# First batch's filter loop without weight conversions: six weight pieces joined in the first quads, first rows read back in two parts

## The chip, the cores and the metric

The kernel runs on one core of a Trainium2 chip. The metric is the device time of one execution in microseconds (us), as the median of several runs. A profile of one further execution comes with it; its times are counted from its first instruction.

## What is computed

The reference mixes each sequence with a filter in the frequency domain and passes the result through a two-layer network with ELU between the layers:

```python
x: (8, 3008, 256)   filt_r, filt_i: (1505, 256)
X = np.fft.rfft(x, axis=1)
y = np.fft.irfft(X * (filt_r + 1j * filt_i)[None], n=3008, axis=1)
h = y.reshape(24064, 256) @ w_in                      # w_in (256, 2048)
g = np.where(h > 0.0, h, np.exp(np.minimum(h, 0.0)) - 1.0)
out = (g @ w_out).astype(np.float32)                  # w_out (2048, 256)
```

The weights w_in and w_out are float64 in memory; the kernel turns them into float32 itself.

## The kernel before

**Batches, units and quads.** The sequence transform of a batch is written as small matrix products (3008 = 47 x 64) with transfers through DRAM between its stages. The network is computed in items (batch b, sixth m of its rows, quarter q of the hidden width): 8 x 6 x 4 of them. One turn of the last loop, here called a quad and numbered i, does the first layer of item i (seven "up" steps, `up_steps`) and the second layer of item i-1 (seven "down" steps, `down_steps`) in an interleaved order that is written out as a string of U and D. Both layers use a seven-product scheme for a 2x2 block product, so each weight quarter also needs four sums of its blocks (`w_sums`). The transform of batch b+1 is spread over the quads of batch b by a hand-written plan: `at(quad, place, fn, ...)` puts a call into a quad at place 2 (after the third step of its first half), place 0 (between the halves) or place 1 (at its end). Each engine runs its own instructions in program order, so a call stands in front of everything that the same engine is given later.

**The opening.** Batch 0 has nothing to overlap with, so it has its own code. Six `a_first` calls do its first transform; eight groups g of four `t_first` transposes, `b_first` and `bi_first` do the rest. `b_first(g)` makes two products on TensorE (PE) into two of the four PSUM banks psM (L329), then runs four products with the filter on VectorE (DVE, `products`, L333 to L336). `bi_first(g)` makes the inverse products (also L329) into psO and two ScalarE (ACT) evictions (L361, L362) into one of two buffers of `t3f`. `y_write_first(g)` (L369) writes that buffer to the DRAM tile `yds[0]`. In turn g of the loop, PE is given `b_first(g)`, `bi_first(g-2)` and, for g below 4, `t_first(g+4)`. When all eight are written, `y_read(0, 0)` (L466) reads the first rows, and `n_unit(0, 0)` (L479, L481) and `n_sums` (L505 to L508) make the input of quad 0.

**The weights.** There are 16 pieces k, four for each quarter q = k // 4: pieces 4q and 4q+1 are w_in, 4q+2 and 4q+3 are w_out. Quad i needs w_in of quarter i in its up steps; the down steps of quarter q run in quad q+1. A piece passes through `w_fetch` (DMA of the float64 words), `w_split` (two DVE operations, L699 and L700, mantissa and exponent bits), `w_float` (four ACT operations, L707, L708, L715, L716), `w_join` (three or four DVE operations, L722, L724, then L729 or L735) and, after the second of a pair, `w_sums` (four DVE operations, L743 to L746). `wtmp` holds two sets of temporaries, for even and for odd pieces.

Before the change pieces 0 to 6 are converted ahead of the loop over g. Inside it stand the float steps of 7 to 11, the joins of 7, 8, 9 and the splits of 8 to 11; in turn 7 follow the joins of 10 and 11 and the splits of 12 and 13; behind the loop, around `y_read`, the floats of 12 to 14, the split of 14 and the joins of 12 and 13. The join of 14 comes after `n_sums(0, 0)`, and piece 15 is converted in quads 0 to 3 of the plan.

**Queues.** GpSimd (POOL) issues the filter reads `ff<-fd` (L318) and most weight fetches, and after them, with no wait on the quads themselves, one memset (L211) and the filter copies `f_pairs` (L771 to L775) from DRAM to DRAM. SyncE (SP) issues the y writes and reads and, behind them, the rows of batch 1 (L202 to L213).

**In the quads.** `keep` (L541, ACT) copies a sum out of the PSUM bank phs, and the next up step adds into the same bank. `add` (L538, DVE) reads a bank and a kept copy; the fourth up step s4 adds into bank phd only after the DVE has read it for g["b22"]. `elu_exp` is L547 and L548 on ACT, `elu_max` is L552 on DVE, and four sums close the item (L588 to L592, DVE). `x_unit` (L219, L220, DVE) at place 0 of quads 2, 3 and 4 prepares batch 1.

Of the kernel before, what the change touches and what calls it, by code (L numbers as in the profile page):

```python
# [130 lines left out]
def kernel(  # L131
# [220 lines left out]
    def bi_first(g):  # L352
        s = ss.pop((0, g))
        t = t3s[0, g] = t3f[:, g % 2]
# [108 lines left out]
    def y_read(b, m, queues=(nc.sync, nc.sync)):  # L463
        t = t4s[b, m] = t4p.tile([P, 4, D], FP32, tag="t4", name="t4")
        for p in range(4):
            queues[p % 2].dma_start(t[p * 32:p * 32 + 32, :, :], yds[b][:, p * H + 4 * m:p * H + 4 * m + 4, :])  # L466

# [201 lines left out]
    def w_fetch(k, queue=nc.gpsimd):  # L669
# [6 lines left out]
        elif k in (6, 7, 8, 9):  # L676
            wd = xp.tile([P, 2, 2, D], FP32, tag="xc", name="wd").rearrange("p k u d -> p (k u d)")
        else:
            wd = fbufs[{5: 0, 12: 1, 13: 2, 14: 0, 15: 1}.get(k, k)].rearrange("p c u d -> p (c u d)")
# [14 lines left out]
    def w_split(k):  # L694
        m, e, c = wtmp[k % 2 if k < 15 else 0]
# [6 lines left out]
    def w_float(k, part=None):  # L702
        m, e, f, l = wts[k]
        if part == 1:
            return w_power(e)

        nc.scalar.activation(out=l, in_=wds[k][:, :, 0], func=AXT.Identity, scale=2.0 ** -52)  # L707
        nc.scalar.activation(out=f, in_=m, func=AXT.Identity, scale=2.0 ** -20, bias=1.0)  # L708
        if part is None:
            w_power(e)  # L710

    def w_power(e):

        ef = e.bitcast(FP32)
        nc.scalar.activation(out=ef, in_=e, func=AXT.Relu, scale=-8.0, bias=edges[:, 0:1])  # L715
        nc.scalar.activation(out=e, in_=ef, func=AXT.Relu, scale=-1.0, bias=edges[:, 1:2])  # L716

    def w_join(k):
# [17 lines left out]
        if j % 2 == 1 and k < 15:  # L736
            w_sums(k)
# [39 lines left out]
    with tc.manual_schedule():  # L777


        with tc.tile_pool(name="boot", bufs=1) as bp:  # L780
# [8 lines left out]
            t3f = t3p.tile([P, 2, 4, D], FP32, tag="t3", name="t3")  # L789
# [10 lines left out]
            for c in range(3):  # L800
# [8 lines left out]
                        [t1p.tile([P, XC, D], FP32, tag="t1", name="wfl").rearrange("p (a b) d -> p a (b d)", a=2)])  # L809
            for i, v in enumerate((1151.0 * 2 ** 23, 255.0 * 2 ** 23)):  # L810
# [30 lines left out]
            for g in range(NG):  # L841
                f_read_first(g, ff[:, g])
                if 3 <= g < 5:
                    w_fetch(g + 7)
            for k in (12, 13, 14):
                w_fetch(k)
            w_split(7)
            w_join(6)
            for g in range(4):
                t_first(g)  # L850
            for g in range(NG + 2):
# [7 lines left out]
                if g < 5:  # L859
                    w_float(g + 7)  # L860
                if g < 3:
                    w_join(g + 7)
                    w_split(g + 8)
                if g == 2:
                    w_split(11)
# [138 lines left out]
```

## Time and profile before

| what | value |
|---|---|
| median of 3 runs (lowest to highest) | 2607.95 us (2606.2 to 2610.34) |
| the profiled execution, its span | 2609.69 us, 2607.9 us |
| mean granted TensorE clock | 0.991 |
| busy share of the span: PE, DVE, ACT, POOL | 98%, 78%, 59%, 7% |
| first product of the filter loop (PE, L329) | 47.89 us |
| last product of the filter loop ends | 86.94 us |
| last eviction (ACT, L362) ends | 89.22 us |
| reads of the first rows issued (SP, ACT) | 92.28 us |
| first product of n_unit (PE, L479) | 96.84 us |
| first product of quad 0, 1, 2, 3, 4 | 100.39, 107.54, 121.09, 134.53, 148.10 us |

A line of the timeline has start, duration, engine, line and operation, output and input tiles, shapes and a count; brackets hold the idle time of that engine just before it and what ended it. A line of the windows has a stretch, then for PE, PE's weight loads (PEld), DVE, ACT and POOL the busy time and number of instructions, then the granted clock (1.00 is full speed), the share of the 16 DMA engines and GB/s. A line of the waits has who waited for whom, the total, the number of times and the longest. PE does one float32 product in two recorded passes.

### The profile page before, as it was taken

To read this page: it belongs to the slowest core of one execution; us is meant where nothing else is said; L and a number is where in the kernel's file an instruction comes from. 1 tells how busy PE (TensorE), PEld (TensorE's weight loads), DVE (VectorE), ACT (ScalarE), POOL (GpSimd) and SP (SyncE) were. 2 spreads that over 40 slices of the span, in tenths; PEclk is the share of its full clock that TensorE was granted. 3 is DMA by queue.
4 is the path that set the end of the run, shared out by engine and by line. 5 is a ranking of instruction groups with operands and counts; after the bars stand their busy time and mean duration, and the time that the engine had idled before them with its cause. 6 is when DMAs were issued, how large, how long until landed. Compare 5 with 4: busy or idle time off the path is not lost.

```text
span 2607.9 us, 39668 instructions
## 1 busy us (share of the span) xinstructions
PE 2549.2 (98%) x14460; PEld 2204.1 (85%) x14460; DVE 2046.0 (78%) x3538; ACT 1546.1 (59%) x2713; POOL 169.6 (7%) x333
## 2 busy tenths in 40 slices
PE   6799999999999999999999999999999999999998
PEld 4688889888898888988889888888888888898887
DVE  6878886788867888778876888778887688866666
ACT  7665655666556655665556556565655655555554
POOL 5100100010000000000000000000010001000000
PEclk8899999999999999999999999999999999999999
DMA  9663213422243231433215231243223322120010
GB/s 275 179 173 73 69 30 96 124 69 58 52 117 93 57 77 46 114 83 75 63 41 145 68 86 37 74 124 85 57 49 81 85 65 69 36 50 20 21 29 17
DMA packets 228834, 206.37 MB, mean 79 GB/s; under 512 B 130962, under 2 KB 194674, under 8 KB 228640
## 3 DMA queue, kind: packets, MB, share of 16 engines
q1 hardware_dynamic: 211328, 166.87, 26.2%
q0 software_dynamic: 15856, 36.25, 5.1%
q8 instruction: 114, 1.87, 0.3%
q10 hardware_dynamic: 1456, 0.72, 0.1%
q14 instruction: 80, 0.66, 0.1%
HBM read 131.87 MB, written 78.17 MB: 81 GB/s over the span
## 4 chain that ended last, share of the span: by engine, by line
PE 89%; DVE 6%; DMA 2%; ACT 1%; issue 1%; POOL 0%; DVEq 0%; ACTq 0%; POOLq 0%
PE po L612 41%; PE phs L530 23%; PE phd L530 12%; PE pha L530 6%; PE psn L479 3%; PE psa L233 1%; PE pf L382 1%; PE pv L445 1%; DVE g L538 1%; DVE g L552 1%; DMA fd<-in_filt_i_dram 1%; DMA t<-in_moe_w_out_dram 0%; ACT e L548 0%; ACT e L547 0%; DMA fd<-in_filt_r_dram 0%
## 5 line engine op out<-in xcount | busy, mean ns | idle before, releaser
L612 PE MATMUL po<-g,wo 128*128 128x256 f32 (+1 forms) x5376 | 1313.0, 376 | 0.0
L612 PEld LDWEIGHTS po<-g,wo 128*128 128x128 f32 x5376 | 1012.1, 190 | 163.2 <-issue 47.4
L541 ACT ACTIVATE g<-phs 128x512 f32<-128x512 f32 (+1 forms) x576 | 338.9, 588 | 766.9 <-PE phs L530 766.9
L538 DVE TENSOR_TENSOR g<-phd,g 128x512 f32<-128x512 f32 (+1 forms) x384 | 259.5, 676 | 302.9 <-ACT e L548 205.4
L548 ACT ACTIVATE e<-e 128x512 f32<-128x512 f32 (+1 forms) x768 | 477.2, 621 | 24.4
L530 PE MATMUL phs<-y,wi 128*128 128x256 f32 (+1 forms) x1536 | 388.8, 376 | 0.5
L530 PE MATMUL phs<-ys,wi 128*128 128x256 f32 (+1 forms) x1536 | 387.7, 375 | 1.5 <-ACT g L541 1.5
L552 DVE SCALAR_TENSOR_TENSOR g<-e,g 128x512 f32<-128x512 f32 (+1 forms) x576 | 386.9, 672 | 0.8 <-ACT e L548 0.2
L547 ACT ACTIVATE e<-g 128x512 f32<-128x512 f32 (+1 forms) x576 | 353.4, 614 | 48.7 <-DVE g L538 37.0
L530 PEld LDWEIGHTS phs<-ys,wi 128*128 128x128 f32 x1536 | 291.4, 190 | 35.4 <-ACT g L541 2.5
L530 PEld LDWEIGHTS phs<-y,wi 128*128 128x128 f32 x1536 | 287.6, 190 | 38.6 <-ACT fall L390 3.4
L552 DVE SCALAR_TENSOR_TENSOR g<-e,phs 128x512 f32<-128x512 f32 (+1 forms) x192 | 129.7, 676 | 138.5 <-ACT e L548 138.5
L530 PE MATMUL phd<-ys,wi 128*128 128x256 f32 (+1 forms) x768 | 195.3, 377 | 10.0 <-DVE g L538 10.0
L530 PE MATMUL phd<-y,wi 128*128 128x256 f32 (+1 forms) x768 | 193.7, 375 | 0.0
L530 PE MATMUL pha<-y,wi 128*128 128x256 f32 (+1 forms) x768 | 193.7, 375 | 0.0
L547 ACT ACTIVATE e<-phs 128x512 f32<-128x512 f32 (+1 forms) x192 | 113.0, 588 | 125.3 <-PE phs L530 125.2
L530 PEld LDWEIGHTS phd<-ys,wi 128*128 128x128 f32 x768 | 144.6, 190 | 31.6 <-DVE g L538 15.5
L530 PEld LDWEIGHTS pha<-y,wi 128*128 128x128 f32 x768 | 145.8, 190 | 16.5
L530 PEld LDWEIGHTS phd<-y,wi 128*128 128x128 f32 x768 | 145.8, 190 | 16.5
L323 POOL DMA_DIRECT2D fall<-fp x224 | 110.5, 501 | 702.6 <-DVE r L418 650.2
L538 DVE TENSOR_TENSOR g<-pha,g 128x512 f32<-128x512 f32 (+1 forms) x192 | 129.1, 672 | 25.2 <-PE pha L530 25.1
L592 DVE TENSOR_TENSOR g<-g,g 128x512 f32<-128x512 f32 (+1 forms) x192 | 130.7, 681 | 6.7
(138 smaller groups left out, 2117.2 us busy)
## 6 DMA issues: line engine op xcount, KB each, us to landing
yd<-t SPq DMA_DIRECT2D x127, 192.0 KB
t<-yd SPq DMA_DIRECT2D x190, 128.0 KB
z<-t SPq DMA_DIRECT2D x84, 256.0 KB
fall<-fp POOLq DMA_DIRECT2D x224, 96.0 KB, 2.9
t<-z SPq DMA_DIRECT2D x224, 96.0 KB
out_dram<-o SPq DMA_DIRECT2D x632, 32.0 KB
tn<-tn_t SPq DMA_DIRECT2D x48, 256.0 KB
xc<-in_x_dram SPq DMA_DIRECT2D x84, 128.0 KB
```

The costliest lines, as they stand in the source:

```text
L233: nc.tensor.matmul(p[o:o + 64, u, :], w[r, u, o:o + 64], src[r, u, :], start=True, stop=True)
L323: nc.gpsimd.dma_start(t[32 * a:32 * a + 24].rearrange("p c u d -> p (c u d)"), fp[g, a].rearrange("q c u d -> q (c u d)"))
L382: nc.tensor.matmul(pf[p][1][32 * a:32 * a + 32, js, :], fb[r, v, :], t2[r, js, a, :], start=True, stop=True, tile_position=(32 * p, 32 * a))
L479: nc.tensor.matmul(ps[:, ts(q, P)], t[:, i - 4 * m, ds(dh * P, P)], w[:, i - 4 * m, :], start=True, stop=True)
L530: nc.tensor.matmul(ps[:, a, 0:h], w_in[q][:, COMBO[n], a, :], y[n], start=start and a == 0, stop=True, skip_group_check=True)
L538: nc.vector.tensor_tensor(out=g[o], in0=i0, in1=i1, op=ALU.add)
L541: nc.scalar.activation(out=g[o], in_=i0, func=AXT.Copy)
L547: nc.scalar.activation(out=e, in_=src, func=AXT.Relu, scale=-1.0)
L548: nc.scalar.activation(out=e, in_=e, func=AXT.Exp, scale=-1.0)
L552: nc.vector.scalar_tensor_tensor(out=g[n], in0=es[n], scalar=1.0, in1=src, op0=ALU.subtract, op1=ALU.max)
L592: nc.vector.tensor_tensor(out=g["t4"], in0=g["b21"], in1=g["t2"], op=ALU.subtract)
L612: nc.tensor.matmul(po[i][:, u, 0:h], w_out[q][:, COMBO[n], a, :], g[n][:, a, :], start=q == 0 and a == 0 and n in (1, 3, 6, 4), stop=True, ...
```

## The change

The filter loop keeps only its own work and the float steps of pieces 7 and 8 (in turns 5 and 7). Piece 8 is split before the loop; the joins of 7, 8, 9, the splits of 9 and 10 and the floats of 9 and 10 stand behind it; the splits of 11, 12, 13 and the float of 11 come after `n_sums(0, 0)`. Pieces 10 to 15 are joined in quads 0 to 3, six in place of one, and the float steps are cut so that the plan can place them one by one. Two new sets of temporaries lie over the loop's product buffers `zq` and `rq`. The weight fetches 10 and 11 move behind all filter reads on POOL, and piece 15 is fetched into the first buffer of `t3f`. Groups 6 and 7 are evicted into `t2` in place of `t3f`. The first rows are read in eight pieces on SP in place of four on SP and ACT: first the rows of groups 0 to 6, then those of group 7. Five products into `warm`, whose result is not used, are given to PE behind the loop.

```diff
-        t = t3s[0, g] = t3f[:, g % 2]
+        t = t3s[0, g] = (t2 if g > 5 else t3f)[:, g % 2]
...
+    def y_read_first():
+        t = t4s[0, 0] = t4p.tile([P, 4, D], FP32, tag="t4", name="t4")
+        for k in (slice(0, K2 - 4), slice(K2 - 4, K2)):
+            for p in range(4):
+                nc.sync.dma_start(t[p * 32 + k.start:p * 32 + k.stop, :, :], yds[0][k, p * H:p * H + 4, :])
...
+        elif k == 15:
+            wd = t3s["first"][:, 0].rearrange("p u d -> p (u d)")
...
-        m, e, c = wtmp[k % 2 if k < 15 else 0]
+        m, e, c = wtmp[{12: 2, 13: 3, 15: 2}.get(k, k % 2)]
...
+    def w_float(k, *parts):
+        m, e, f, l = wts[k]
+        ef = e.bitcast(FP32)
+        steps = ((l, wds[k][:, :, 0], AXT.Identity, 2.0 ** -52, 0.0), (f, m, AXT.Identity, 2.0 ** -20, 1.0),
+                 (ef, e, AXT.Relu, -8.0, edges[:, 0:1]), (e, ef, AXT.Relu, -1.0, edges[:, 1:2]))
+        for i in parts or range(4):
+            o, x, func, scale, bias = steps[i]
+            nc.scalar.activation(out=o, in_=x, func=func, scale=scale, bias=bias)
...
-        if j % 2 == 1 and k < 15:
+        if j % 2 == 1 and k < 11:
             w_sums(k)
...
+            for t in (zq, rq):
+                flat = t.rearrange("p a u d -> p a (u d)")
+                wtmp.append([flat[:, 0].bitcast(U32), flat[:, 1].bitcast(U32), flat[:, 2:4]])
...
                 f_read_first(g, ff[:, g])
-                if 3 <= g < 5:
-                    w_fetch(g + 7)
-            for k in (12, 13, 14):
+            for k in range(10, 15):
                 w_fetch(k)
             w_split(7)
             w_join(6)
+            w_split(8)
...
-                if g < 5:
-                    w_float(g + 7)
-                if g < 3:
-                    w_join(g + 7)
-                    w_split(g + 8)
-                if g == 2:
-                    w_split(11)
                 if g >= 2:
                     y_write_first(g - 2, (nc.sync, nc.scalar if g == NG + 1 else nc.sync))
-                if g == 7:
-                    w_join(10)
-                    w_join(11)
-                    w_split(12)
-                    w_split(13)
-            w_float(12)
-            y_read(0, 0, (nc.sync, nc.scalar))
-            w_float(13)
-            w_join(12)
+                if g in (5, 7):
+                    w_float(7 + (g - 5) // 2)
+            y_read_first()
+            w_join(7)
+            w_split(9)
+            w_float(9)
+            w_join(8)
+            w_split(10)
             w_fetch(15)
-            w_split(14)
-            w_float(14)
-            w_join(13)
+            w_join(9)
+            w_float(10)
+            warm = psO.tile([P, 512], FP32, tag="po2", name="warm")
+            for k in range(5):
+                nc.tensor.matmul(warm, w_in[0][:, 0, 0, :], w_in[0][:, 0:2].rearrange("p a b c -> p (a b c)"),
+                                 start=True, stop=True)
...
         n_sums(0, 0)
-        w_join(14)
+        for k in (11, 12, 13):
+            w_split(k)
+        w_float(11)
...
-        for quad, place, fn, *a in ((0, 0, w_split, 15), (1, 1, w_float, 15, 0), (2, 0, w_float, 15, 1), (2, 1, w_join, 15),
-                                    (3, 0, w_sums, 15)):
+        for quad, place, fn, *a in ((0, 2, w_join, 10), (0, 2, w_float, 12, 0, 1, 2), (0, 1, w_join, 11),
+                                    (0, 1, w_float, 12, 3), (0, 1, w_float, 13, 0),
+                                    (1, 2, w_sums, 11), (1, 2, w_float, 13, 1, 2, 3), (1, 0, w_split, 14),
+                                    (1, 1, w_join, 12), (1, 1, w_float, 14, 0, 1),
+                                    (2, 2, w_join, 13), (2, 0, w_split, 15), (2, 2, w_float, 14, 2, 3),
+                                    (2, 1, w_sums, 13), (2, 1, w_float, 15, 0, 1),
+                                    (3, 2, w_join, 14), (3, 2, w_float, 15, 2, 3), (3, 0, w_join, 15),
+                                    (3, 1, w_sums, 15)):
...
-            at(2 + i, 1, nc.vector.memset, fbufs[i], 0.0)
+            at(3 - i, 1, nc.vector.memset, fbufs[i], 0.0)
```

More of the change, by code (lines that the diff above doesn't have):

```diff
@@ L677, in w_fetch @@
             wd = xp.tile([P, 2, 2, D], FP32, tag="xc", name="wd").rearrange("p k u d -> p (k u d)")
+        elif k == 15:
+            wd = t3s["first"][:, 0].rearrange("p u d -> p (u d)")
         else:
-            wd = fbufs[{5: 0, 12: 1, 13: 2, 14: 0, 15: 1}.get(k, k)].rearrange("p c u d -> p (c u d)")
+            wd = fbufs[{5: 0, 12: 1, 13: 2, 14: 0}.get(k, k)].rearrange("p c u d -> p (c u d)")
         wd = wds[k] = wd.bitcast(U32).rearrange("p (a w) -> p a w", w=2)
@@ L700, in w_split @@
         nc.vector.tensor_scalar(out=e, in0=hi, scalar1=0x7FF00000, scalar2=None, op0=ALU.bitwise_and)
-    def w_float(k, part=None):
+    def w_float(k, *parts):
         m, e, f, l = wts[k]
[L704 to L712, printed above, removed]
-        ef = e.bitcast(FP32)
-        nc.scalar.activation(out=ef, in_=e, func=AXT.Relu, scale=-8.0, bias=edges[:, 0:1])
-        nc.scalar.activation(out=e, in_=ef, func=AXT.Relu, scale=-1.0, bias=edges[:, 1:2])
+        ef = e.bitcast(FP32)
+        steps = ((l, wds[k][:, :, 0], AXT.Identity, 2.0 ** -52, 0.0), (f, m, AXT.Identity, 2.0 ** -20, 1.0),
[3 more added lines that the diff above has]
+            nc.scalar.activation(out=o, in_=x, func=func, scale=scale, bias=bias)
     def w_join(k):
@@ L788 @@
             pqs = [[rq[:, 2 * i], rq[:, 2 * i + 1], zq[:, 0:2, i], zq[:, 2:4, i]] for i in range(2)]
-            t3f = t3p.tile([P, 2, 4, D], FP32, tag="t3", name="t3")
+            t3f = t3s["first"] = t3p.tile([P, 2, 4, D], FP32, tag="t3", name="t3")
             zt[0] += [bp.tile([P, 16 * ROWS], FP32, name="zt%d" % i) for i in range(2)]
```

## The prediction

> **What bounds the kernel now.** I read the windows of the first 310 us first. From 110 us on PE is busy in every stretch, so time can be won or lost only before that, or by making PE wait later. Three stretches around the filter loop, and the single microseconds in which the clock changes:
>
> ```profile
> 70.00:80.00 10.00, 8.67 (x49) 5.15 (x53) 7.61 (x14) 5.53 (x10) 0.00 (x0) 0.66 0.29 89
> 80.00:90.00 10.00, 6.94 (x60) 4.27 (x51) 9.80 (x19) 4.61 (x9) 0.00 (x0) 1.00 0.60 154
> 90.00:100.00 10.00, 3.16 (x15) 3.19 (x16) 8.70 (x19) 7.84 (x13) 3.59 (x6) 0.56 0.83 208
> ...
> 70.00:71.00 1.00, 0.00 (x0) 0.00 (x0) 1.00 (x3) 0.97 (x2) 0.00 (x0) 0.85 0.90 333
> 91.00:92.00 1.00, 0.00 (x0) 0.00 (x0) 1.00 (x3) 0.97 (x2) 0.00 (x0) 0.59 0.70 224
> 101.00:102.00 1.00, 1.00 (x5) 0.96 (x5) 0.76 (x3) 0.32 (x2) 0.00 (x0) 0.79 1.08 418
> ```
>
> In 90 to 100 PE works 3.16 of 10 us, at half clock. An average of 0.85 over a microsecond at full and half speed is a change at 70.7, 0.59 at 91.2, 0.79 back at 101.4. So the clock fell 2.2 us after PE's last work in one gap (68.5) and 4.2 us in the other (86.9), and came back 4.6 us after work resumed (96.84).
>
> Next the timelines of PE, ACT and DVE, for the waits in that part:
>
> ```profile
> 58.96 1.07 PE L329 MATMUL psr<-tf,once 48*64 48x512 f32 x2 [1.34 <-DVE rq L334]
> 71.33 1.96 PE L329 MATMUL psr<-t,once 48*64 48x512 f32 x2 [2.83 <-DVE rq L334]
> 96.84 3.75 PE L479 MATMUL psn<-tn,t 128*128 128x128 f32 x16 [9.91 <-DMA t<-yd]
> ```
>
> ```profile
> 88.14 0.60 ACT L361 ACTIVATE t<-po 128x512 f32<-128x512 f32 x1 [2.26 <-DMA yd<-t]
> ```
>
> PE waits for the filter products (L334), DVE itself being without a pause from 56.96 to 74.86: between the products stand the splits, joins and sums. At the end an eviction waits for its buffer, and the first product of `n_unit` for the rows that came back.
>
> Last, what room DVE has in the quads, and what POOL waits for:
>
> ```profile
> 115.79 0.62 DVE L538 TENSOR_TENSOR g<-phd,g 128x448 f32<-128x448 f32 x1 [2.62 <-PE phd L530]
> ...
> 155.72 0.69 DVE L538 TENSOR_TENSOR g<-phd,g 128x512 f32<-128x512 f32 x1 [2.27 <-PE phd L530]
> ```
>
> ```profile
> POOL fall L687 <- DVE we L722: 30.3, 2, 29.4
> ```
>
> **1. The loop: -11.9 us.** Removed from between the products are the joins of 7 to 9, their sums and the splits of 8 to 11. DVE then has four products per group, 4 x 0.60 = 2.4 us. PE has the group's `b_first` and `bi_first`; in the undisturbed part a group takes 82.40 - 79.83 = 2.57 us (starts of L333). So PE is late next, by 0.17 us a group. Until 57.62 (end of a `t_first`) nothing changes. Then come five groups of 2.57, one `t_first` of 1.08, and the two last `bi_first`, two thirds of a group each (16 of 24 recorded passes): 12.85 + 1.08 + 3.44 = 17.4, so PE ends at 75.0 in place of 86.94. This needs full clock, which held until 60.7 before, and fell after waits that now go. Filter reads are no limit: before, the last was issued at 59.38 and took 7.7 at the median, so 67.1; its products now start near 69.9.
>
> **2. The last eviction: -0.2 us.** The buffer wait (2.26) goes, since groups 6 and 7 use `t2`, whose last reader ends before. In its place stands ACT's float of piece 8: group 5's evictions end near 72.6, the four steps take 2.5 (71.96 to 74.50), four evictions 1.95: 77.05, 2.05 after PE. Before it was 89.22 - 86.94 = 2.28.
>
> **3. Out to DRAM and back: +1.4 us.** Before: 96.84 - 89.22 = 7.62. After, three terms follow each other. The write: 3.1 by the row 89.22 to 92.28, 4.0 by the write that the eviction at 88.14 waited for (from 84.15); I take 3.5. Eight pieces are issued on SP alone; the first four can go while group 7 is being written, but the last four stand behind them, at 0.40 each (two in 0.79): 1.6. The read: 3.9 (92.78 to 96.70) for 128 KB beside other loads; the late pieces are an eighth of the rows, so this is the upper end; the lower end is nothing saved but the data, which I can't price, and I keep 3.9. Sum 9.0, bounds 6.6 (3.1, 1.6 and half the read) and 9.5. PE then starts `n_unit` at 77.0 + 9.0 = 86.0 in place of 96.84. The joins of 7 to 9 and their sums (about 11 us of DVE from 72.3) hide in here.
>
> The Trainium skill (DMA: Bandwidth & Descriptors, rules for kernel authors) says that splitting a transfer over disjoint partitions is not worth it, since the halves share the same engines. By it the split itself brings nothing, and the sum would keep the old 7.6; here the two parts have different waits, which that rule does not weigh, and no run here shows it yet.
>
> **4. The five idle products: 0.** Two passes of 512 columns each, at 0.216 per 256 (0.86 for four): 5 x 0.86 = 4.3 us, starting when po2 is evicted, 75.7, so ending at 80.0. That leaves 6.0 us to 86.0. The clock fell 2.2 and 4.2 us after work ended, so `n_unit` is cold again, as before. If it held, `n_unit` would take 1.8 and not 3.75: -2.0.
>
> The skill's page TensorE: Matmul & The Clock Gate (Why this matters) sets the limit for a gap near 3 us. The two falls above lie on both sides of that; by the rule too a gap of 6.0 is cold, and the products buy nothing.
>
> **5. Quad 0: +3.3 us.** ACT carries the float of 11 ahead of the first `keep`, and its second step waits for the split of 11, which DVE does after `n_sums`. Counted from `n_unit`'s start (before: 96.84): evictions end at +4.3, `n_sums` +5.4, split +6.1, ACT's four steps (0.58, then 0.52, 0.74, 0.62 from +5.8) +7.7, `keep` +8.2. Before, that `keep` ended at +5.6. Then three steps of 12, 1.8, to +10.0; the second `keep` ends at +10.5 (before 104.06, +7.2). From there 3.96 to the `elu_max` at 108.02 as before: +14.5 in place of +11.2. PE stands behind each `keep`, since the next step adds into the same bank.
>
> **6. DVE in quads 0 to 4: +5.9 us.** From that `elu_max` to the add at 155.72 DVE gets in addition two w_out joins of 2.07 (135.19 to 137.26), two w_in joins of 2.01 (93.05 to 95.06), sums of 11 and 13 at 1.6, splits of 14 and 15 at 0.67: 12.7. The join and the sums of 15 were there already. DVE's idle time in that stretch is 2.62 + 0.71 + 1.04 + 1.32 + 0.16 + 0.16 + 2.27 = 8.3; of it some 1.5 stays (an exponential in quad 1, the end of quad 4, gaps at the memsets). So 6.8 is absorbed and 5.9 shows, as PE waiting before s4 in quads 2 and 3, where join, split and `x_unit` (2.65) stand ahead of the add. From quad 5 on DVE has 4.5 us to spare again (wait at 169.67) and nothing more is lost. Bounds: 12.7 - 8.3 = 4.4 and, if only the two long waits serve, 12.7 - 4.9 = 7.8. ACT's steps moved into the quads lie in waits of 1.7 to 2.0 us for phs and cost nothing more; without that cover each is 0.5 to 0.75.
>
> Wait-free edits (temporaries over `zq` and `rq`, memsets exchanged, piece 15 in `t3f`) cost 0: the buffers' next users come in quad 6 or later, and `f_read`, which needs the memsets, has its products at 194.
>
> **Sum:** -11.9 - 0.2 + 1.4 + 0 + 3.3 + 5.9 = -1.5 us. On the profiled execution, 2609.69, that is 2608.2; the median of the runs shown, 2607.95, lies 1.7 lower, and on it I predict 2606.5. A measurement here tells some 0.2% (5.2 us) from no change.
>
> **Rivals.**
>
> *The opening is worth more (chance 0.25).* The clock holds (-2.0), the way back takes 6.6 (-2.4), the quads absorb all 8.3 (-1.5): -7.4, 2600.6. For it: late reads are small. Against: the gap of 6.0.
>
> *POOL's copies meet the rows (0.12, slower).* POOL waited 29.4 us for a join before fetching piece 15. Now it waits only for group 4's write, near 75, then fetches 512 KB and issues the first filter copies near 77, which before came at 95.89. They meet the last writes and the reads. Copies of that kind took about 7 us from issue to landing (fp<-fd 6.4 and 7.0). If write and read take 7 each, the way is 7.0 + 1.6 + 7.0 = 15.6, 6.6 more: +5.1, 2613.1. It decides once the way is longer than 10.5. Against: DMA share of 0.29 and 0.60 in 70 to 90, so there is room.
>
> *The change doesn't do what it says: the loop stays slow (0.08).* The weight fetches (10 to 14, 2.5 MB) now run beside the y writes; if a write takes the 7.7 of the filter reads, made while the engines were full, a buffer comes free after 7.7 + 1.0 for two groups, 4.35 a group in place of 2.57, for four groups: +7.1, so +5.6, 2613.6. Against: the write named in step 3 took 4.0.
>
> **How the numbers follow.** My forecast has 0.55, with a range of its own from 2602.5 to 2610 (terms 3 and 6). The range of 8 in 10 goes from 2599.5, past the first rival, to 2612, short of the two slow ones. Faster by over 0.2% (below 2602.7): most of the first rival and a little of the forecast, 0.27. Slower (above 2613.2): half of the two slow rivals and some of the unknown, 0.12. The rest 0.61.
>
> **What would show it.** Right: L333 starts every 2.6 us from group 3, PE's loop ends near 75, `n_unit` starts near 86 at half clock, `keep` of quad 0 waits for the float of 11, PE waits 2 to 3 us for DVE (L538) in quads 2 and 3. Wrong: evictions (L361) waiting for yd writes in turns 6 and 7; a gap over 10.5 between the last eviction and `n_unit`; a clock of 1.00 in `n_unit`; no PE waits in quads 2 and 3.

## The result, and the profile after

The changed kernel takes 2615.49 us in the median (2613.33 to 2617.86, 10 runs), the kernel before 2608.82 (2605.86 to 2611.80, 10 runs). The ratio is 1.0026, with a 95% interval from 1.0016 to 1.0036: slower by 6.7 us, where 1.5 us less was forecast and the range ended at 2612. The profiled execution of the changed kernel took 2617.86 us, at the upper end of its runs, with a span of 2616.1 (before 2607.9).

The opening did come forward, but by half of what was forecast, and the first quads gave back more than that. Three distances that follow each other show it: from the first product of the filter loop to the end of the last eviction (*loop*), from there to the first product of `n_unit` (*way*), and from there to the first product of quad 5 (*quads*), after which the two traces run alike (13.01 us to the next quad in both).

| distance, us | before | forecast | after | miss |
|---|---|---|---|---|
| loop (start at 47.89, after: 47.98) | 41.33 | 29.2 | 31.67 | +2.5 |
| way | 7.62 | 9.0 | 12.04 | +3.0 |
| quads | 64.79 | 74.0 | 77.60 | +3.6 |
| sum | 113.74 | 112.2 | 121.31 | +9.1 |

The windows of the same three stretches, after (line numbers are now those of the changed kernel: `b_first` and `bi_first` L329, `n_unit` L485, up steps L536, `add` L544, `keep` L547):

```profile
70.00:80.00 10.00, 8.82 (x59) 3.44 (x53) 9.41 (x20) 9.58 (x18) 0.69 (x2) 1.00 0.53 134
80.00:90.00 10.00, 2.79 (x7) 0.95 (x5) 5.55 (x11) 4.96 (x8) 2.88 (x5) 0.90 0.82 252
90.00:100.00 10.00, 5.38 (x25) 4.85 (x26) 3.75 (x11) 4.34 (x8) 3.99 (x7) 0.76 0.85 281
```

The loop now runs at full clock (1.00 where it was 0.66). But 80 to 90 is a hole: PE has 2.79 us of work, all of it in the idle products, DVE 5.55, while the DMA engines are busier than before (0.82 against 0.60). The chain of waits says on what the time went:

```profile
79.67 8.28 DMA yd<-t
...
89.26 2.25 DMA ta<-ta_t
91.69 3.50 PE psn L485 x16
```

The last y write takes 8.28 us; four read issues on SP follow, then the landing of the last rows, 2.25 us (put down to ta, which SP issued right behind them; `n_unit` doesn't read ta). What else was on the DMA engines is in POOL's timeline:

```profile
79.31 1.06 POOL L695 DMA_DIRECT2D t<-in_moe_w_out_dram  x2 [17.65 <-ACT t L361]
80.41 0.52 POOL L211 MEMSET xc<- 32x512 f32 x1
80.87 0.89 POOL L772 DMA_DIRECT2D fp<-fd  x1
81.75 0.64 POOL L773 DMA_DIRECT2D fp<-fd  x1
```

The last weight fetch and the first filter copies, which came at 94.04 and 95.89 before, go out within 2 us of the last y write. While that write runs (79.65 to 87.95), the DMA engines are at 0.93; during the two writes that the forecast priced (84.15 to 88.14 and 89.22 to 92.28 in the kernel before) they were at 0.66 and 0.51. In the loop itself one eviction waits for a y write (ACT's timeline):

```profile
66.52 0.60 ACT L361 ACTIVATE t<-po 128x512 f32<-128x512 f32 x1 [3.87 <-DMA yd<-t]
```

In `n_unit` and the quads, PE's timeline shows these waits:

```profile
91.69 3.49 PE L485 MATMUL psn<-tn,t 128*128 128x128 f32 x16 [8.89 <-DMA ta<-ta_t]
...
99.76 1.02 PE L536 MATMUL phs<-ys,wi 128*128 128x224 f32 x4 [2.93 <-ACT g L547]
...
101.88 1.86 PE L536 MATMUL phs<-ys,wi 128*128 128x224 f32 x4 [1.09 <-ACT g L547]
...
111.19 1.26 PE L536 MATMUL phs<-ys,wi 128*128 128x224 f32 x4 [1.92 <-ACT g L547]
...
134.31 1.02 PE L536 MATMUL phd<-ys,wi 128*128 128x224 f32 x4 [2.74 <-DVE g L544]
...
150.80 1.02 PE L536 MATMUL phd<-ys,wi 128*128 128x224 f32 x4 [1.16 <-DVE g L544]
```

The waits for `keep` in quad 0 and for `add` in quads 2 and 3 are those that steps 5 and 6 named. The wait of 1.92 in quad 1 they did not name: step 6 let ACT's float steps there cost nothing. Nor did they name what shows in the duration of the second product, 1.86 in place of 1.02, and in single microseconds behind three of the waits:

```profile
102.00:103.00 1.00, 1.00 (x3) 0.93 (x4) 0.36 (x2) 0.00 (x0) 0.34 (x1) 0.50 1.00 198
112.00:113.00 1.00, 1.00 (x5) 0.88 (x4) 1.00 (x2) 0.97 (x3) 0.00 (x0) 0.50 0.00 0
136.00:137.00 1.00, 1.00 (x4) 0.89 (x4) 0.96 (x2) 0.94 (x3) 0.00 (x0) 0.50 0.00 0
```

PE is busy without a pause, at half clock.

Steps 5 and 6 of the prediction meet at the `elu_max` of quad 0, and step 6 ends at an `add` in quad 4. These rows of DVE's timeline measure them (the first is from the kernel before; the `add` there came at 155.72):

```profile
108.02 0.62 DVE L552 SCALAR_TENSOR_TENSOR g<-e,phs 128x448 f32<-128x448 f32 x1 [0.57 <-ACT e L548]
```

```profile
107.16 0.62 DVE L558 SCALAR_TENSOR_TENSOR g<-e,phs 128x448 f32<-128x448 f32 x1 [0.71 <-ACT e L554]
...
163.38 0.69 DVE L544 TENSOR_TENSOR g<-phd,g 128x512 f32<-128x512 f32 x1 [1.44 <-PE phd L536]
```

From `n_unit` to that `elu_max` it is 15.47 us in place of 11.18, so +4.3 where +3.3 was forecast; from there to the `add` 56.22 in place of 47.70, so +8.5 where +5.9 was forecast.

### The profile page after: what moved, and what is told of

Same layout as the page of the kernel before. It is cut to its first block, busy times and chain, and to the rows that moved or that the text cites. A ratio compares the mean times of both kernels' runs of the same rounds, so it can differ in the third digit from the quotient of the medians.

```text
span 2616.1 us, 39702 instructions
## 1 busy us (share of the span) xinstructions
PE 2553.3 (98%) x14470; PEld 2204.5 (84%) x14470; DVE 2045.2 (78%) x3538; ACT 1545.6 (59%) x2713; POOL 169.3 (6%) x333
## 3 DMA queue, kind: packets, MB, share of 16 engines
HBM read 131.87 MB, written 78.17 MB: 80 GB/s over the span
## 4 chain that ended last, share of the span: by engine, by line
PE 89%; DVE 6%; DMA 2%; ACT 2%; issue 1%; SPq 0%; DVEq 0%
PE po L618 41%; PE phs L536 23%; PE phd L536 12%; PE pha L536 6%; PE psn L485 3%; PE psa L233 1%; PE pf L382 1%; PE pv L445 1%; DMA xc<-in_x_dram 1%; DVE g L544 1%; DVE g L558 1%; DMA x<-in_x_dram 0%; ACT e L554 0%; DMA yd<-t 0%; ACT e L553 0%
## 5 line engine op out<-in xcount | busy, mean ns | idle before, releaser
L547 ACT ACTIVATE g<-phs 128x512 f32<-128x512 f32 (+1 forms) x576 | 338.8, 588 | 763.6 <-PE phs L536 763.6
L544 DVE TENSOR_TENSOR g<-phd,g 128x512 f32<-128x512 f32 (+1 forms) x384 | 259.5, 676 | 302.2 <-ACT e L554 206.7
L536 PE MATMUL phs<-ys,wi 128*128 128x256 f32 (+1 forms) x1536 | 388.8, 376 | 5.9 <-ACT g L547 5.9
L536 PE MATMUL phs<-y,wi 128*128 128x256 f32 (+1 forms) x1536 | 388.3, 375 | 0.6
L536 PEld LDWEIGHTS phs<-ys,wi 128*128 128x128 f32 x1536 | 292.1, 190 | 40.1 <-ACT g L547 7.0
L536 PEld LDWEIGHTS phs<-y,wi 128*128 128x128 f32 x1536 | 287.3, 190 | 38.7 <-ACT fall L390 3.4
L536 PE MATMUL phd<-ys,wi 128*128 128x256 f32 (+1 forms) x768 | 195.3, 377 | 13.2 <-DVE g L544 13.2
L536 PE MATMUL phd<-y,wi 128*128 128x256 f32 (+1 forms) x768 | 194.4, 376 | 0.0
L536 PE MATMUL pha<-y,wi 128*128 128x256 f32 (+1 forms) x768 | 193.8, 375 | 0.0
L536 PEld LDWEIGHTS phd<-ys,wi 128*128 128x128 f32 x768 | 144.5, 190 | 35.3 <-DVE g L544 19.2
L536 PEld LDWEIGHTS phd<-y,wi 128*128 128x128 f32 x768 | 146.4, 191 | 16.6
L536 PEld LDWEIGHTS pha<-y,wi 128*128 128x128 f32 x768 | 145.8, 190 | 16.8 <-ACT y L487 0.2
L544 DVE TENSOR_TENSOR g<-pha,g 128x512 f32<-128x512 f32 (+1 forms) x192 | 129.0, 672 | 26.6 <-PE pha L536 25.8
```

Source lines behind the costliest of these rows:

```text
L536: nc.tensor.matmul(ps[:, a, 0:h], w_in[q][:, COMBO[n], a, :], y[n], start=start and a == 0, stop=True, skip_group_check=True)
L544: nc.vector.tensor_tensor(out=g[o], in0=i0, in1=i1, op=ALU.add)
L547: nc.scalar.activation(out=g[o], in_=i0, func=AXT.Copy)
```

## The experiments

**Theory after the result:** the way is long because POOL's transfers share the DMA engines with the y write and the reads; the quads lose some 6 us to the float of 11 ahead of the first `keep` (half of it the clock) and some 6 to joins and sums on DVE. **Rivals:** the way is set by SP's eight issues, or by the write alone; the quads are set by DVE's load only, or by ACT's float steps only. The kernels were run in four sets; ratios are to the kernel before on the same chip (medians 2609.5 to 2610.4). All distances are from the one profiled execution of each kernel.

| kernel | loop | way | quads | median, us | ratio [95%] |
|---|---|---|---|---|---|
| e1_gate | 30.53 | 8.32 | 77.04 | 2613.36 | 1.0009 [1.0000, 1.0018] |
| e2_idle | 31.85 | 11.69 | 71.17 | 2610.24 | 1.0001 [0.9992, 1.0010] |
| e3_nowarm | 30.03 | 11.67 | 79.14 | 2617.15 | 1.0027 [1.0017, 1.0037] |
| e4_parts | 39.97 | 7.44 | 65.24 | 2608.45 | 0.9995 [0.9986, 1.0004] |
| e5_both | 30.36 | 8.32 | 71.21 | 2609.43 | 1.0001 [0.9992, 1.0009] |
| e6_fill | 29.87 | 13.41 | 74.78 | 2613.68 | 1.0017 [1.0008, 1.0026] |
| e7_float | 33.42 | 10.82 | 71.49 | 2610.93 | 1.0009 [1.0000, 1.0018] |
| e8_late14 | 29.93 | 8.22 | 71.75 | 2608.33 | 0.9992 [0.9983, 1.0001] |
| e9_spread | 29.83 | 8.39 | 70.71 | 2605.78 | 0.9983 [0.9974, 0.9992] |
| e10_copies | 32.31 | 10.69 | 77.85 | 2615.60 | 1.0020 [1.0011, 1.0028] |
| e11_fetch12 | 29.84 | 8.24 | 77.06 | 2613.35 (one run) | |
| e12_onepart | 29.84 | 8.67 | 77.73 | 2613.52 | 1.0014 [1.0005, 1.0022] |
| e13_nojoin | 31.08 | 11.39 | 65.82 | 2604.18 | 0.9981 [0.9972, 0.9990] |
| e14_pool | 29.83 | 8.12 | 69.77 | 2603.55 | 0.9975 [0.9966, 0.9984] |

How to read it: the loop's first product came between 46.9 (e2_idle) and 51.0 us (e5_both), though nothing that runs ahead of it was changed in any but e4_parts; whether that goes with the kernel or with the execution is open. So distances are compared, not absolute times. The changed kernel on this basis, 1.0026 x 2609.8, is about 2616.5; "under the changed kernel" below is meant against that.

### The way

**e1_gate**: the last fetch and all filter copies wait for `n_unit`, through a memset on POOL.

```diff
+        first = t4s[0, 0]
         n_unit(0, 0)
+        nc.gpsimd.memset(first[0:32, 0, 0:1], 0.0)
+        w_fetch(15)
```

> The changed kernel, with one thing put off: POOL first waits until PE has read the first rows for n_unit (a memset of one column of that tile, 32 partitions, behind n_unit), and only then fetches piece 15 and issues the filter copies. Theory A (POOL's transfers, set free early, slow the last y write, 8.28 us from issue to landing): the write takes about 4 us again, n_unit starts near 87.5 in place of 91.69, the whole is 4 us faster than the changed kernel, near 2611.5. Rival (the write is slow by itself, 1 KB pieces over 48 partitions, and eight reads on one queue cost their issue): n_unit starts within 1 us of 91.69, time near 2615.

Measured: the way falls from 12.04 to 8.32, the median to 2613.36, some 3 us under the changed kernel (4 were expected). Its timeline (PE, SP and POOL):

```profile
86.49 3.75 PE L485 MATMUL psn<-tn,t 128*128 128x128 f32 x16 [5.17 <-DMA xc<-in_x_dram]
```

```profile
79.87 3.73 SPq L472 DMA_DIRECT2D t<-yd  x8
```

```profile
88.65 0.09 POOL L886 MEMSET t<- 32x1 f32 x1 [28.16 <-PE psn L485]
```

SP issues all eight reads without a pause from 79.87 to 83.60 (in the changed kernel it stood between the fourth and the fifth: 7.72 us for the eight). The loss of the way is POOL's transfers: 3.7 us here, and in all kernels with the gate the way is 8.1 to 8.7, in those of the changed opening without it 10.8 to 13.4.

**e10_copies**: e1_gate, but the last fetch goes out early, as in the changed kernel.

```diff
+            w_fetch(15)
             w_join(9)
...
         nc.gpsimd.memset(first[0:32, 0, 0:1], 0.0)
-        w_fetch(15)
```

> As e1_gate, but only the filter copies wait for n_unit; the last weight fetch (512 KB) goes out in the way to DRAM and back, as in the changed kernel. Theory A (the copies fill the engines: with the fetch alone the way stays near 8.3 to 9 us): n_unit 8.3 to 9.2 after the last eviction, time as e1_gate, about 2613. Theory B (the fetch, 0.5 MB at some 280 GB/s = 1.9 us, and what stands queued behind it lengthen the way): the way is 10 to 12 us, time nearer to the changed kernel's 2616.5.

Measured: way 10.69, median 2615.60. Theory B: the 512 KB fetch is most of it; with it alone the last y write takes 7.24 us. What the copies add can't be told, since 10.69 lies at the edge of the ungated ways.

**e12_onepart**: e1_gate with the rows read in one part.

```diff
-            y_read_first()
+            y_read(0, 0, (nc.sync, nc.sync))
```

> As e1_gate, with the first rows read in one part of four pieces, all on SP, in place of two parts of four. Theory (SP's issues set the end of the way: the eight reads go out without a pause at 0.47 us each, so the first part is not ahead of the second by anything but SP's own time): four issues fewer, the way is 6.8 to 7.5 us in place of 8.3, n_unit 1 to 1.5 us earlier. Rival (the late part is small and lands in 2.3 us, a whole read of 128 KB pieces takes 3.9 us as before the change; the split pays for its issues): the way is 8.3 +- 0.4 us.

Measured: way 8.67 against 8.32, medians 2613.52 and 2613.36, the rival's case. Reading in two parts brings nothing that can be measured here, and costs nothing: in e1_gate the early part goes out only 1.7 us after the last eviction (79.87 against 78.17), and the late part follows it without a pause. The Trainium skill's advice against splitting (DMA: Bandwidth & Descriptors, rules for kernel authors) agrees with this pair.

This run also has the pieces of a gated way in its chain of waits:

```profile
79.60 4.11 DMA yd<-t
...
85.20 2.91 DMA t<-yd
```

The write takes 4.11 us with the DMA engines at 0.72. Without the gate the chains that hold it show 8.28 (the changed kernel), 6.17 (e2_idle), 9.81 (e6_fill) and, with the fetch alone, 7.24 (e10_copies).

**e3_nowarm**: the changed kernel without the five idle products.

```diff
-            warm = psO.tile([P, 512], FP32, tag="po2", name="warm")
-            for k in range(5):
-                nc.tensor.matmul(warm, w_in[0][:, 0, 0, :], w_in[0][:, 0:2].rearrange("p a b c -> p (a b c)"),
-                                 start=True, stop=True)
```

> The changed kernel without the five products into warm. Theory A: they end at 82.8, 8.9 us before n_unit, which is at half clock with them and without them: no difference, within 1 us of 2615.5. Rival (they keep the clock up into quad 0): without them n_unit and quad 0 lose 2 us or more.

Measured: 2617.15, the same as the changed kernel; `n_unit` is at half clock with and without them. In the single profile quads are 1.5 longer (the first products of quad 0 are cold too), which the medians, some 0.7 apart, don't show.

**e4_parts**: the kernel before, with groups 6 and 7 in `t2` and the read in two parts; all conversions where they were.

```diff
-        t = t3s[0, g] = t3f[:, g % 2]
+        t = t3s[0, g] = (t2 if g > 5 else t3f)[:, g % 2]
...
-            y_read(0, 0, (nc.sync, nc.scalar))
+            y_read_first()
```

> The kernel before, with two parts of the change alone: groups 6 and 7 evicted into t2, and the first rows read in two parts on SP. All weight conversions stay where they were. Theory A: the eviction's wait of 2.26 us goes, the read's landing is shorter by 1.6 (2.3 in place of 3.9) but is issued in 1.3 us more; n_unit starts 2 to 3 us earlier, and as the quads are untouched the whole is 2 to 3 us faster than before, near 2606. Rival (DVE's joins behind the loop, which reach to 99.8, set the start of quad 0 anyway): no gain, 2608 to 2609.

Measured: 2608.45, ratio 0.9995, so no difference that the measurement can tell; in the profile the loop is 1.4 and the way 0.2 shorter, the quads 0.5 longer. The interval reaches down to 0.9986, or 3.7 us, so the 2 to 3 us that were expected are not ruled out either. Without the move of the conversions these two parts bring nothing that shows.

### The loop

**e8_late14**: e5_both (below) with the fetch of piece 14 behind the gate too.

```diff
-            for k in range(10, 15):
+            for k in range(10, 14):
...
+        w_fetch(14)
         w_fetch(15)
```

> As e5_both, with the fetch of piece 14 also behind n_unit. Theory (the eviction of group 2 in the filter loop waits 3.9 us for a y write that shares the DMA engines with weight fetches 10 to 14): with 0.5 MB less in that stretch the wait falls by 1 us or more, the loop ends near 77, n_unit starts about 1 us earlier than in e5_both. Rival (the write is slow for another reason, such as the filter reads, or fetches 10 to 13 are enough to fill the engines): the wait stays at 3.9 +- 0.3, n_unit within 0.3 us of e5_both.

**e11_fetch12**: e1_gate with the fetches of 12, 13 and 14 behind the gate too.

```diff
-            for k in range(10, 15):
+            for k in range(10, 12):
...
-        w_fetch(15)
+        for k in range(12, 16):
+            w_fetch(k)
```

> As e1_gate, with only the fetches 10 and 11 ahead of the loop's end; 12 to 15 go out behind n_unit. Only the loop is read in this run: the splits of 12 and 13 now wait for their pieces, which delays quads 0 and 1 by up to 10 us. Theory (the eviction of group 2 waits 3 to 4 us for the y write of group 0 because that write shares the DMA engines with weight fetches): with 1 MB less than in e8_late14 the wait (3.2 us there, 4.15 with all five fetches) falls below 2 us, and the last eviction ends 12 us or less after that eviction's start. Rival (the filter reads or the write itself set it): still 3 us or more.

Measured: the wait of group 2's eviction for the y write is 4.15 us in e5_both, 3.23 in e8_late14, and gone in e11_fetch12, where the eviction waits for PE:

```profile
66.13 0.60 ACT L361 ACTIVATE t<-po 128x512 f32<-128x512 f32 x1 [1.81 <-PE po L329]
```

So the weight fetches do slow the y writes. This rests on e11_fetch12 alone, a single run: the step from 4.15 to 3.23 says nothing, since kernels with all five fetches ahead have waits from 2.92 (e13_nojoin) to 4.15. But the loop is 29.83 to 29.93 in six kernels, e11_fetch12 among them, and in the other five a wait of 3.1 to 3.8 us in group 2 costs nothing; the loop is longer where a second wait follows (e7_float 2.98 and 3.57: 33.42; e10_copies 3.33 and 3.34: 32.31; e2_idle 3.64 and 2.57: 31.85). The changed kernel's 31.67 is 1.8 us longer than these six; there too the next eviction waits again, 2.16 us (at 69.76), but the view puts that down to PE, whose products for it had ended at 66.95, so that its cause is not shown. e6_fill has the same opening and 29.87, and the changed kernel's median is 2.4 below its profiled execution, so those 1.8 us need not be in its other executions. What makes the writes slower in one than in another is open.

### The quads

**e2_idle**: the splits of 11 to 13, the floats of 11 and 12 and the joins of 10 and 11 go ahead of `n_unit`, where DVE and ACT stood idle.

```diff
+        for k in (11, 12, 13):
+            w_split(k)
+        w_float(11)
+        w_join(10)
+        w_float(12)
+        w_join(11)
         n_unit(0, 0)
         n_sums(0, 0)
-        for k in (11, 12, 13):
-            w_split(k)
-        w_float(11)
...
-        for quad, place, fn, *a in ((0, 2, w_join, 10), (0, 2, w_float, 12, 0, 1, 2), (0, 1, w_join, 11),
-                                    (0, 1, w_float, 12, 3), (0, 1, w_float, 13, 0),
+        for quad, place, fn, *a in ((0, 1, w_float, 13, 0),
```

> The changed kernel, with some conversions taken out of the quads and put ahead of n_unit, where DVE (86.4 to 94.4) and ACT (85.1 to 93.8) wait for the rows: the splits of 11 to 13, the floats of 11 and 12, the joins of 10 and 11. Theory A (what stands in the quads on ACT and DVE is what makes the changed kernel slower; 12.8 us between n_unit and quad 5): quad 0 loses its 4.3 us, DVE's stretch to quad 4 another 2, together about 6 us less, near 2609. Rival (the quads are slow because the clock is low or because transfers are late, not because of these instructions): less than 2 us gained, above 2613.5.

**e7_float**: only the three splits and the float of 11 go ahead; joins 10 and 11 and float 12 stay in quad 0.

```diff
+        for k in (11, 12, 13):
+            w_split(k)
+        w_float(11)
         n_unit(0, 0)
         n_sums(0, 0)
-        for k in (11, 12, 13):
-            w_split(k)
-        w_float(11)
```

> The changed kernel with only the splits of 11, 12 and 13 and the float of 11 ahead of n_unit; joins 10 and 11 and float 12 stay in quad 0. Theory (step 5 of the prediction: the float of 11 ahead of the first keep costs about 3 us by itself, and DVE's joins the rest): elu_max of quad 0 at n_unit + 12, as before the change about, the quads lose some 9 in place of 12.8 us, and the time is 3 us lower than the changed kernel, about 2613, ratio to before 1.0015. Rival (DVE's total load sets the quads, and keep's delay is made up within its queue): elu_max comes earlier but DVE is late by as much in quads 2 and 3, quad 5 at n_unit + 76 or later, time within 1 us of the changed kernel.

Measured: quads 71.17 (e2_idle) and 71.49 (e7_float) against 77.60; medians 2610.24 and 2610.93, some 6 us under the changed kernel. The splits and the float of 11 are all of the gain, 6.1 us, twice what was expected of them. The two joins (some 4 us of DVE) cost nothing in quad 0, so DVE's load is not what sets that quad. PE's waits in e7_float:

```profile
99.39 1.02 PE L536 MATMUL phs<-ys,wi 128*128 128x224 f32 x4 [1.08 <-ACT g L547]
...
107.33 1.02 PE L536 MATMUL phs<-ys,wi 128*128 128x224 f32 x4 [2.07 <-ACT g L547]
...
128.82 1.10 PE L536 MATMUL phd<-ys,wi 128*128 128x224 f32 x4 [2.75 <-DVE g L544]
```

The wait of 2.93 in quad 0 is gone, and the products behind the waits in quads 0 and 1 take 1.02: the clock holds until the wait in quad 2.

**e6_fill**: the changed kernel, with three products without use in quad 0 and two in quad 1, so that PE is busy in its waits for `keep`.

```diff
+        def fill(n):
+            i, ps = bank("fill", (P, 512))
+            for k in range(n):
+                nc.tensor.matmul(ps, w_in[0][:, 0, 0, :], w_in[0][:, 0:2].rearrange("p a b c -> p (a b c)"),
+                                 start=True, stop=True)
+            banks.append(i)
+
+        at(0, 2, fill, 3)
+        at(1, 2, fill, 2)
```

> The changed kernel with five products whose result is not used, three in quad 0 and two in quad 1, each behind the third up step. Theory (in quad 0 PE's waits for ACT let the clock fall to half in two stretches, 101.6 to 104.9 and 111.8 to 115.3 in the changed kernel's profile, and these cost some 1.6 us each on the way to elu_max): with the gaps filled the clock stays at 1.00 there, elu_max of quad 0 comes 2 to 3 us earlier and the time is 2 to 3 us lower than the changed kernel, about 2613.5. Rival (DVE's queue sets the quads, PE's clock is hidden behind it): the clock rows change but quad 5 starts at n_unit + 77 to 78 as in the changed kernel, same time, or up to 4 us more if the extra products themselves stand in the way (five of 0.86 at full clock).

Measured: quads 74.78 in place of 77.60, median 2613.68: 2.8 us by both, from work that computes nothing. The `elu_max` of quad 0 comes 1.1 us earlier, not 2 to 3; the rest of the gain shows in quad 1. In the stretches that were at half clock:

```profile
104.00:105.00 1.00, 1.00 (x7) 0.87 (x5) 0.00 (x0) 0.50 (x2) 0.00 (x0) 1.00 0.99 234
112.00:113.00 1.00, 1.00 (x8) 1.00 (x6) 1.00 (x2) 0.97 (x2) 0.00 (x0) 1.00 0.12 28
```

So of the 6.1 us that e7_float gained, some 2.8 are the clock behind the waits, and 3.3 the waits themselves. About half of the clock's part is not the price of the float of 11: quad 1 is 1.5 us shorter in e7_float (14.76 in place of 16.25), although the same wait stands in it (2.07 and 1.92), because the clock held there; the last section shows on what that hangs. Up to the first product of quad 1 the splits and the float cost 15.14 - 10.50 = 4.6 us.

**e13_nojoin**: e7_float without the joins of 12 to 15 and the sums of 13 and 15; POOL fills that quarter of the weights with zeros.

```diff
+            nc.gpsimd.memset(w_in[3], 0.0)
+            nc.gpsimd.memset(w_out[3], 0.0)
             w_fetch(15)
...
-            at(quad, place, fn, *a)
+            if (fn, a[0]) not in ((w_join, 12), (w_join, 13), (w_join, 14), (w_join, 15), (w_sums, 13), (w_sums, 15)):
+                at(quad, place, fn, *a)
```

> The kernel of e7_float without the joins of pieces 12 to 15 and the sums of 13 and 15; the fourth quarter of the weights is filled with zeros by POOL in place of them, so that quarter is left out of the result. Splits and float steps stay. DVE has 4 x 2.04 + 2 x 1.6 = 11.4 us less in quads 1 to 3. Theory (DVE's load sets the quads): PE's waits of 2.75 and 1.16 us for DVE in quads 2 and 3 go, the clock stays at 1.00, quad 5 at n_unit + 65 to 66 in place of 71.5 (before: 64.8), time 5 to 6 us under e7_float, near 2605.5, ratio 0.998. Rival (ACT's float steps, which hold back keep and the exponentials, set them): PE waits for ACT instead, quad 5 at n_unit + 69 or later, time within 3 us of e7_float.

Measured: quads 65.82, median 2604.18. PE has no wait for DVE in quads 2 and 3; DVE waits for PE in quad 3 instead:

```profile
136.78 0.62 DVE L544 TENSOR_TENSOR g<-phd,g 128x448 f32<-128x448 f32 x1 [2.02 <-PE phd L536]
```

The joins and sums cost 71.49 - 65.82 = 5.7 us; those of piece 15, which the kernel before has in its quads too, are among them. What is left to the kernel before, 65.82 - 64.79 = 1.0, is a balance: quads 0 and 1 are 0.7 and 1.2 longer, where PE still waits for `keep` (1.04 and 2.07), and quad 3 is 0.9 shorter. So the rival (ACT sets the quads) is out for quads 2 and 3, and has about 1.2 us in quad 1.

### Versions that put both together

**e5_both**: e1_gate and e2_idle in one.

> The changed kernel with both earlier edits together: the last weight fetch and the filter copies wait for n_unit, and splits 11 to 13, float 11, joins 10 and 11 and float 12 stand ahead of n_unit in place of quads 0 and 1. Theory (the way out to DRAM and back is lengthened by POOL's transfers, and the conversions in the quads cost some 6 us on top; the two prices are independent): n_unit starts near 86.5, quad 5 near 86.5 + 71.2 = 157.7, against 161.6 before and 169.3 after the change, so 4 us under the kernel before, about 2606, ratio 0.9985. Rival (the two edits buy the same idle time, so that only the larger counts): n_unit at 86.5 but joins and floats now push it or quad 0 back, quad 5 near 161.5, ratio 1.000 as with the second edit alone.

Measured: way 8.32 and quads 71.21, as the theory had it, so the two prices are independent; but in its profiled execution the loop started at 51.0, 3.1 us later than before, and the median is 2609.43, not 2606: the expected time failed by about as much as that start, for which no cause was found; whether the other executions behind the median started as late is not known.

**e9_spread**: e8_late14 with DVE's steps spread over quads 0 to 2.

```diff
-        for quad, place, fn, *a in ((0, 1, w_float, 13, 0),
-                                    (1, 2, w_sums, 11), (1, 2, w_float, 13, 1, 2, 3), (1, 0, w_split, 14),
-                                    (1, 1, w_join, 12), (1, 1, w_float, 14, 0, 1),
-                                    (2, 2, w_join, 13), (2, 0, w_split, 15), (2, 2, w_float, 14, 2, 3),
-                                    (2, 1, w_sums, 13), (2, 1, w_float, 15, 0, 1),
-                                    (3, 2, w_join, 14), (3, 2, w_float, 15, 2, 3), (3, 0, w_join, 15),
+        for quad, place, fn, *a in ((0, 2, w_sums, 11), (0, 1, w_join, 12), (0, 1, w_float, 13, 0),
+                                    (1, 2, w_float, 13, 1, 2, 3), (1, 0, w_split, 14),
+                                    (1, 1, w_join, 13), (1, 1, w_float, 14, 0, 1),
+                                    (2, 2, w_float, 14, 2, 3),
+                                    (2, 1, w_split, 15), (2, 1, w_sums, 13), (2, 1, w_float, 15, 0),
+                                    (3, 2, w_join, 14), (3, 2, w_float, 15, 1, 2, 3), (3, 0, w_join, 15),
```

> The kernel of e8_late14 with the DVE steps of quads 0 to 2 spread otherwise: sums 11 in quad 0 (idle DVE of 2.70 us there), join 12 at the end of quad 0, join 13 at the end of quad 1, split 15 at the end of quad 2. Theory (what is left of the loss in the quads is DVE work that stands ahead of the add in quad 2: PE waits 2.75 us there, and the clock falls to half for some 3.3 us behind that wait, 1.6 to 1.9 us more): the wait in quad 2 falls under 1 us, the clock stays at 1.00, quad 5 at n_unit + 67 to 69 in place of 71.7, time 2604 to 2605.5, ratio 0.998 to before. Rival (DVE has no room until quad 4, so the wait only moves on to quad 3, and with it the fall of the clock): PE waits 2.5 us or more in quad 3, quad 5 at n_unit + 71, time within 1 us of e8_late14.

Measured: 2605.78, ratio 0.9983, under both kernels; quads 70.71. Each side had a part: the wait in quad 2 is gone, one as long stands in quad 3 (the rival), and yet the clock holds behind it:

```profile
138.41 1.02 PE L536 MATMUL phd<-ys,wi 128*128 128x224 f32 x4 [2.62 <-DVE g L544]
```

```profile
139.00:140.00 1.00, 1.00 (x7) 0.84 (x5) 0.94 (x2) 0.97 (x2) 0.00 (x0) 1.00 0.96 294
```

**e14_pool**: e9_spread with the memsets of the filter buffers on POOL.

```diff
-            at(3 - i, 1, nc.vector.memset, fbufs[i], 0.0)
+            at(3 - i, 1, nc.gpsimd.memset, fbufs[i], 0.0)
```

> The kernel of e9_spread with the two memsets of the filter buffers (128x1024, 0.91 us each with 0.16 idle before them, at the ends of quads 2 and 3) on POOL in place of DVE. Theory (DVE is without a pause through quads 2 and 3): PE's wait of 2.62 us in quad 3 falls to some 1.5, quad 5 comes 1 to 2 us earlier against n_unit (68.7 to 69.7 in place of 70.7), time 1 to 2 us under e9_spread, ratio 0.9975 to 0.998. Rival (POOL's memset runs several us and holds DVE up, or the filter reads behind it come late): no gain, or a loss.

Measured: the wait in quad 3 is 1.61, quads 69.77, median 2603.55, ratio 0.9975. DVE is without a pause through quads 2 and 3, and what is taken from it there comes off: one memset stood ahead of that `add` (at 129.78), 1.07 us with its idle time, and the wait is 1.01 shorter. The intervals of the two ratios overlap, so the medians alone would not show it.

```profile
137.92 1.02 PE L536 MATMUL phd<-ys,wi 128*128 128x224 f32 x4 [1.61 <-DVE g L544]
```

## Why the prediction was wrong, by its steps

**1 and 2, the loop and the last eviction (-12.1; measured -9.7).** The mechanism was right: the products follow each other at PE's rate, at full clock. Of the miss of 2.5, 0.7 is a mis-sized stretch (an undisturbed loop is 29.83, the forecast was 29.16): in e9_spread the last two `bi_first` take 2.2 and 2.3 us in place of 1.7, and the evictions behind them less than forecast. The other 1.8 go with the second late eviction. The forecast had waits for y writes in the rival "the loop stays slow" (0.08). It came at a quarter of its price, and in five of the fourteen profiled kernels with this loop a first wait of 3.1 to 3.8 us was caught up.

**3, the way (+1.4; measured +4.4).** The failing term is the write: 3.5 was taken from rows in which the DMA engines were at 0.66 and 0.51; it took 8.28, with the engines at 0.93. The reads were mis-sized the other way: 2.25 in place of 3.9. The rival "POOL's copies meet the rows" named the transfers, the place and the point from which it decides (10.5; the way was 12.04), and e1_gate shows it: held back, they cost the way nothing, and in e12_onepart the write takes 4.11. The argument against it, the room on the DMA engines in 70 to 90, was read from a stretch into which the change itself moved new traffic. POOL's wait for a join had been the gate that kept these transfers out, and the change took it away.

**4, the idle products (0).** Right: e3_nowarm takes the same time, and `n_unit` is cold either way.

**5, quad 0 (+3.3; measured +4.3 at its `elu_max`).** The waits were right: the two copies end at `n_unit` + 8.0 and + 10.1, forecast 8.2 and 10.5. The step that failed is "from there 3.96 to the `elu_max` as before": it took 5.33, because it counted the products behind the waits at full clock, and they ran at half clock up to 105.01. With the waits filled (e6_fill) the `elu_max` comes 1.1 earlier, with the splits and the float moved (e7_float) 4.5. The forecast asked whether the clock would hold in `n_unit`, and of the waits that it added itself it did not ask.

**6, DVE in quads 0 to 4 (+5.9; measured +8.5, beyond its upper bound of 7.8).** The waits for DVE in quads 2 and 3 came as forecast (2.74 and 1.16), and e13_nojoin shows that joins and sums make them. Two things failed. "ACT's steps moved into the quads ... cost nothing more": in quad 1 PE waits 1.92 us for `keep` behind them, which makes the quad 1.2 longer even where the clock holds (e7_float, e13_nojoin). And the clock again: it fell for one step behind that wait, which made quad 1 another 1.5 longer (2.7 in all), and for one behind the wait in quad 2, which is 4.6 longer with a wait of 2.74 in it; a step at half clock, 1.7, is nearly all of the rest.

**The sum.** The misses of 2.5, 3.0, 1.0 and 2.6 are 9.1, all of one sign; from -1.5 they lead to +7.6 in the profile (121.31 - 113.74) and +6.7 in the medians. The rivals were priced one at a time; two of the slow ones came in part together, and with the clock on top, and a range built from single cases did not reach that.

## What to carry to other kernels

When a wait on a spare engine goes, list what was queued behind it: transfers that a wait used to hold back will start at the earliest moment, here within 2 us of the write that the critical path needs, and an artificial wait (a memset of one column, 0.09 us) is a cheap way to hold them. Work moved out of a loop is best put where its engine is idle and nothing hangs on it: the same splits and float cost 4.6 us or more behind `n_sums` and nothing that shows ahead of `n_unit`. A wait of 2 us that you add to TensorE is to be priced with the clock behind it, up to 1.7 us more each time, and it is worth looking for the version without it.

## What the runs showed of the hardware

The granted clock changes only at whole steps of 3.41 us. Worked out from windows of half a microsecond, the changed kernel's clock fell and rose at 87.94, 94.77, 101.59, 105.01, 111.83, 115.24, 135.72 and 139.14: 2, 2, 1, 2, 1, 6 and 1 steps. The kernel before (60.46, 63.87, 70.70, 77.52, 91.18, 101.42) and the other profiles fit their own such grid, whose place differs from execution to execution. In the sixteen profiles, from 35 to 2600 us, it fell from full speed after every step in which PE was busy for less than 0.415 of the time, and stayed after every step with more than 0.44, but for two of 0.57 in the filter loop (the kernel before and e4_parts). Between these it fell five times and stayed three times. So a wait counts by how it lies on the grid: 1.92 us within one step made the clock fall (at 111.83), 2.07 us of which 1.58 lay in one step did not (e7_float), and of the 2.62 us in e9_spread, which did not either, 1.93 lay in one step, which puts that step (PE busy for 0.44 of it) right at the limit. This also explains why the falls that the forecast read as 2.2 and 4.2 us after the last work lay so far apart. One step at half clock costs PE half of 3.41, 1.7 us. The Trainium skill (TensorE: Matmul & The Clock Gate, The HAM clock gate) tells of such a free-running window of 3413 ns; the length agrees with these runs, but where it asks for an idle window, here one in which PE was busy for two fifths was enough (0.44 and 0.41 ahead of the falls at 111.83 and 135.72).
